# Conv weights of a lag stored side by side, v staged in filter slots, and a new job order, in a fused attention and long-convolution kernel

## The chip, the cores and the metric

The kernel runs on one core of one Trainium2 chip. The metric is the device time of one execution in microseconds (us). I call the engines PE (matmuls; PEld is its weight load), DVE (vector), ACT (scalar), POOL and SP, as the profile does. PSUM is the memory, in banks, that the matmuls write. The chain is the profile's path of work and waits that ended last. On one core an execution counts as slow when it lies over 1.5% above the fastest of the same kernel. A ratio is the mean time of one kernel's fast runs over the mean of the other's fast runs of the same rounds, so it is not quite the ratio of the medians that I quote beside it.

## The reference

Two independent parts, side by side in the output:

```python
# A: attention, S = 2048, D = 512, 32 heads of 16
qkv = (x @ wqkv).reshape(B, S, 3, H, Dh)
p = softmax(q @ k.T * Dh ** -0.5);  a = (p @ v) @ wo
# B: a short conv of 4 taps on k, times v, then a causal conv over the whole sequence, per channel
kv = short_conv(k, shift_k) * v
y = irfft(rfft(kv, 2 * S) * rfft(ssm_k, 2 * S))[:S] + kv * ssm_D
b = q * y
return concatenate([a, b], axis=-1)
```

## The kernel before

A Python scheduler emits one static program. Step T is one exponential on ACT over 2 or 3 banks of scores (741 steps). Between them PE does scores, p@v, projections and pieces of the conv; DVE computes 213 further score blocks by a polynomial (four passes each: FX, then EH, EH, EH or PTD) and empties PSUM.

The long conv is a matmul. For a channel, the 128 rows of `WR` hold the filter shifted by 0 to 63 places, once for each of two channels; the weights of a lag are up to 32 columns of `KV` (products of short conv and v). Four channels go to four column groups of the array at a time:

```python
KVF = sb("KV", [128, 2, 2 * NB, C // 2])          # channel innermost: a lag's weights are 512 bytes apart
KV = KVF[:, :, :, :].rearrange("p r (e h) u -> p r e h u", h=2)
...
# conv_lags: one lag, four channels c
ins = e.matmul(PS[32 * c:32 * c + 32 - 2 * q, BGB, 128 * kk:128 * kk + w],
               lhsT=KVF[:, lag % 2, 2 * q:32, 4 * od + c],
               rhs=WR[:, rows[c], w0:w0 + w],
               start=(n == 0), stop=(n == NLAG - 1), tile_position=(0, 32 * c))
...
# evac_unit, kind "kv": v was loaded into KV itself, and is multiplied in place
dst = KV[64 * p:64 * p + 64, i // 4, 4 * (i % 4):4 * (i % 4) + 4, p, 128 * c:128 * c + 128]
e.tensor_tensor(dst, src, dst, ALU.mult)           # src is PSUM; 32 of these, 64 x 512 each
```

`WR` has five slots of two channels. When a group of four channels is done, two slots are refilled, each by two transfers of 512 KB:

```python
def load_wr():
    while wr_free and wr_next[0] < 2 * NOCT:
        (i, dep), x = wr_free.pop(0), wr_next[0]
        ...                                          # cut
        for h in range(2):
            h_wr[x] = dma(sp, d_wr[i], WR[64 * h:64 * h + 64, 2 * i:2 * i + 2, :], src, [h_kzw[0], dep])
```

The softmax here doesn't subtract the row's maximum and nothing guards it: scores larger than these inputs give would overflow.

## Time and profile before

| | before |
|---|---|
| time, median of 4 | 987.3 us (982.4 to 991.3) |
| ACT, DVE, PE busy | 93%, 88%, 83% |
| mean PE clock granted | 0.944 |
| mean length of a DVE pass EH<-EH,FX | 781 ns |
| mean length of a product (L399) | 733 ns |

The lines themselves stand in the prediction. For the stages I count exponentials: step 60 ends at 82.4 us, step 184 at 230.9 us, step 740 at 978.6 us. So three stages: up to step 60 (projections alone), steps 60 to 184 (the products are made here) and steps 184 to 740 (attention with the conv, the long stage). From the trace I also add up, for each stage, the time at half PE clock, and the *fetch stalls*: gaps over 0.6 us in which PE has nothing in progress and for which a packet of the instruction queue ran in the 3 us before or during the gap. Such sums come from one profiled execution of each kernel.

### The profile page before, as it was taken

How to read it: one execution, taken by the hardware profiler on the slowest of the kernel's cores; microseconds unless marked ns; L12 is line 12 of the kernel's file. 1: busy time of each engine (PE TensorE's matmuls, PEld its weight loads, DVE VectorE, ACT ScalarE, POOL GpSimd, SP SyncE). 2: the span in 40 equal slices, each digit the busy share in tenths (PEclk: the TensorE clock that was granted, in tenths of full speed). 3: DMA queues.
4: the chain of work that ended last, by engine and by line, in shares of the span. 5: the costliest groups of instructions: out<-in, count | busy, mean ns of one | idle time of the engine just before them, and what ended most of it. 6: DMA issues, size and time to landing. Idle time of an engine off the chain costs nothing.

```text
span 985.5 us, 29568 instructions
## 1 busy us (share of the span) xinstructions
PE 814.5 (83%) x13348; PEld 376.9 (38%) x13389; DVE 865.7 (88%) x1330; ACT 912.0 (93%) x746; POOL 32.3 (3%) x35
## 2 busy tenths in 40 slices
PE   7888989888888888788887878877778888888877
PEld 2223233444344434344343344444444444333332
DVE  3238799999989999889899898999989999999993
ACT  5998799999989999989898899999989999999997
POOL 7000000000000000000000000000000000000000
PEclk9997599999989999989799799999989999999999
DMA  9990003538788988977788798887978977776502
GB/s 262 246 203 1 1 8 97 114 87 197 169 184 200 192 180 178 205 166 172 163 191 178 167 235 201 188 182 178 206 162 189 195 169 171 175 155 145 121 2 65
DMA packets 68013, 155.14 MB, mean 157 GB/s; under 512 B 31152, under 2 KB 33200, under 8 KB 67504
## 3 DMA queue, kind: packets, MB, share of 16 engines
q1 hardware_dynamic: 62624, 145.12, 66.4%
q0 software_dynamic: 1808, 6.29, 2.3%
q8 instruction: 106, 1.74, 0.8%
q10 hardware_dynamic: 3456, 1.84, 0.7%
q14 instruction: 19, 0.16, 0.1%
HBM read 142.61 MB, written 6.42 MB: 151 GB/s over the span
## 4 chain that ended last, share of the span: by engine, by line
ACT 46%; DVE 24%; PE 21%; issue 6%; SPq 1%; DMA 1%; ACTq 0%
ACT PT L555 46%; DVE EH L598 11%; PE PS L544 8%; PE PS L812 5%; PE PS L637 5%; DVE FX L591 4%; DVE PTD L603 4%; DVE KV L399 2%; PE PS L361 1%; DVE QT L386 1%; DVE DT L701 1%; SPq L221 1%; DMA WR<-in_B_ssm_D_dram 1%; PE PS L754 1%; PE PS L340 1%
## 5 line engine op out<-in xcount | busy, mean ns | idle before, releaser
L555 ACT ACTIVATE PT<-PS 128x1536 bf16<-128x1536 f32 (+1 forms) x741 | 908.9, 1424 | 61.5 <-PE PS L544 59.0
L544 PE MATMUL PS<-QT,KTo 32*128 32x512 bf16 x2048 | 316.9, 403 | 95.8 <-ACT PT L555 71.3
L598 DVE SCALAR_TENSOR_TENSOR EH<-EH,FX 128x512 f32<-128x512 f32 x426 | 320.3, 781 | 0.3
L812 PE MATMUL PS<-WR,KV 128*26 128x128 bf16 (+8 forms) x8192 | 286.2, 245 | 36.5 <-issue 35.0
L812 PEld LDWEIGHTS PS<-WR,KV 128*22 128x22 bf16 (+7 forms) x8192 | 231.9, 152 | 122.6 <-issue 100.6
L637 PE MATMUL PS<-PT,VAF 128*32 128x512 bf16 x1835 | 213.4, 409 | 13.0 <-issue 6.5
L591 DVE TENSOR_SCALAR FX<-PS 128x512 f32<-128x512 f32 x213 | 160.0, 751 | 30.5 <-PE PS L544 29.7
L544 PEld LDWEIGHTS PS<-QT,KTo 32*128 32x128 bf16 x2048 | 74.2, 91 | 268.7 <-ACT PT L555 216.1
L603 DVE SCALAR_TENSOR_TENSOR PTD<-EH,FX 128x512 uint16<-128x512 f32 x213 | 163.2, 771 | 0.3
L598 DVE SCALAR_TENSOR_TENSOR EH<-FX 128x512 f32<-128x512 uint16 x213 | 160.6, 774 | 0.1
L637 PEld LDWEIGHTS PS<-PT,VAF 128*32 128x32 bf16 x1835 | 49.7, 94 | 139.4 <-issue 121.4
L1012 PE MATMUL PS<-IDN,ZW 128*32 128x256 bf16 (+3 forms) x245 | 81.0, 331 | 0.7 <-DVE QN L845 0.4
L637 PE MATMUL PS<-PTD,VAF 128*32 128x512 bf16 x213 | 65.9, 407 | 0.0
L701 DVE STREAM_TRANSPOSE DT<-PS 128x512 f32<-128x512 f32 x31 | 23.1, 745 | 18.4 <-PE PS L637 18.2
L410 DVE CAST VAF<-PS 128x512 bf16<-128x512 f32 x16 | 11.1, 691 | 28.3 <-PE PS L369 28.3
L1012 PEld LDWEIGHTS PS<-IDN,ZW 128*32 128x32 bf16 x245 | 27.3, 112 | 5.8 <-issue 5.3
L399 DVE TENSOR_TENSOR KV<-PS,KV 64x512 bf16<-64x512 f32 x32 | 23.5, 733 | 3.7 <-PE PS L361 3.1
L386 DVE TENSOR_SCALAR QT<-PS,MASK 128x512 bf16<-128x512 f32 x30 | 21.4, 752 | 5.9 <-PE PS L340 5.7
L221 POOL DMA_DIRECT2D out_dram<-OUTA x12 | 7.1, 588 | 576.7 <-DVE OUTA L763 576.7
L369 PE MATMUL PS<-WKV,xT 128*128 128x512 bf16 x59 | 18.1, 391 | 6.0 <-DVE VAF L410 4.9
L754 PE MATMUL PS<-WKV,OTN 128*128 128x512 bf16 x50 | 16.9, 393 | 3.8 <-issue 1.9
L391 DVE CAST KTo<-PS 128x512 bf16<-128x512 f32 (+1 forms) x16 | 11.7, 732 | 8.8 <-PE PS L349 8.8
(63 smaller groups left out, 233.7 us busy)
## 6 DMA issues: line engine op xcount, KB each, us to landing
WR<-kz_scratch SPq DMA_DIRECT2D x256, 512.0 KB, 8.7
kz_scratch<-WR SPq DMA_DIRECT2D x1, 2176.0 KB, 8.5
KV<-in_B_v_dram SPq DMA_DIRECT2D x8, 256.0 KB, 6.1
QN<-in_B_q_dram POOLq DMA_DIRECT2D x2, 1024.0 KB, 11.5
out_dram<-QN POOLq DMA_DIRECT2D x2, 1024.0 KB, 7.2
out_dram<-OUTA POOLq DMA_DIRECT2D x12, 128.0 KB, 6.1
QN<-in_B_ssm_k_dram SPq DMA_DIRECT2D x1, 1024.0 KB, 6.2
QT<-in_B_ssm_k_dram SPq DMA_DIRECT2D x1, 1024.0 KB, 8.1
```

What stands on the lines that cost most here:

```text
L386: lambda e, par=par: e.tensor_scalar(QT[:, qb % 2, 2 * o + par, :], PS[:, bank, :], MASK[:, par:par + 1], None, ALU.mult),
L399: h_kvc[c] = hh = urgent(lambda e, dst=dst, src=src: e.tensor_tensor(dst, src, dst, ALU.mult), [h, h_vn[2 * c + i // 4], h_kv0], us=V512)
L544: ins = e.matmul(PS[:, bank, :], lhsT=KTo[32 * s:32 * s + 32, g // 2, kt * 128:(kt + 1) * 128], rhs=QT[32 * s:32 * s + 32, qb % 2, g, :], ...
L555: h_exp[T] = act.op(lambda e: e.activation(PT[:, T % R_PT, 0:n * QB], PS[:, banks[0]:banks[0] + n, :].rearrange("p b f -> p (b f)"), ACT.E ...
L591: h_f = urgent(lambda e: e.tensor_scalar(fx, PS[:, bank, :], FIX_ADD, FIX_HI, ALU.add, ALU.min), [h, h_last.get(i - R_FX)], slack=0.6)
L598: st["h"] = dve.op(lambda e: e.scalar_tensor_tensor(eh, src, (A3, A2, A1)[j], frac, ALU.add, ALU.mult), [st["h"], h_last.get(i - R_EH), h_ ...
L603: lambda e: e.scalar_tensor_tensor(out16, eh, A4, fx, ALU.mult, ALU.add),
L637: ins = e.matmul(dst, lhsT=w, rhs=rhs, start=(k == 0), stop=(k == KT - 1), tile_position=(0, 32 * s))
L701: h_t = urgent(lambda e: e.transpose(out=dt, in_=PS[:, pvb(n), :]), [h] + before, slack=0.1, us=(0.63, 0.751))
L754: ins = e.matmul(PS[:, bank, :], lhsT=OTN[:, (4 * qb + o) % R_O, t * 128:(t + 1) * 128], rhs=WO[:, o, :], start=(o == 0), stop=(o == 3))
L812: ins = e.matmul(PS[32 * c:32 * c + 32 - 2 * q, BGB, 128 * kk:128 * kk + w], lhsT=KVF[:, lag % 2, 2 * q:32, 4 * od + c], rhs=WR[:, rows[c] ...
L1012: pe.op(lambda e: e.matmul(PS[32 * s:32 * s + 32, pvb(n), 0:128 * k], lhsT=ZW[:, :], rhs=rhs, start=False, stop=False, tile_position=(0, 3 ...
```

## The change

The intent: bring a lag's weights next to each other (2 bytes apart instead of 512), so that weight loads are short. v can then no longer be loaded into its place by DMA in useful runs, so it is staged in two of the five filter slots, which come free when the last product is done. The job scheduler was changed with it.

```diff
-    KVF = sb("KV", [128, 2, 2 * NB, C // 2])
-    KV = KVF[:, :, :, :].rearrange("p r (e h) u -> p r e h u", h=2)
+    KVF = sb("KV", [128, C // 2, 2, 2 * NB])
+    KV = KVF[:, :, :, :].rearrange("p u r (e h) -> p r e h u", h=2)
+    VST = WR[:, 6:10, :]...                         # (cut) v, as [64 h, c, r, block, 128]
-    ld = dma(sp, d_kv[2 + 2 * c + r], KV[64 * h:64 * h + 64, r, :, h, 128 * c:128 * c + 128], src, kb=512)
+    ld = dma(sp, d_kv[2 + 2 * c + r], VST[64 * h:64 * h + 64, c, r, :, :], src, kb=512)
-    for h in range(2):                              # two memsets of 64 rows become one of 128
-        h_kv0 = pool.op(lambda e, h=h: e.memset(KV[64 * h:64 * h + 64, :, :, 1 - h, :], 0.0), ...)
+    h_kv0 = pool.op(lambda e: e.memset(KVF[:, :, :, :], 0.0), [h_vaf1], us=(14.0, 14.1))
-    e.tensor_tensor(dst, src, dst, ALU.mult)
+    e.tensor_tensor(dst, src, val, ALU.mult)        # val = the staged v
-    wr_free.extend([(i, h_kzw[0]) for i in range(R_W // 2)])   # at the start: five slots
+    wr_free.extend([(i, h_kzw[0]) for i in range(3)])          # now three
+    wr_free.extend([(3, hh), (4, hh)])              # after the last product
-    lhsT=KVF[:, lag % 2, 2 * q:32, 4 * od + c],
+    lhsT=KVF[:, 4 * od + c, lag % 2, 2 * q:32],
 # job order (N_EARLY is 184; cut to what differs)
+    if N_EARLY - 8 <= T < N_EARLY: return None      # no later job in the last 8 early steps
-    jobs.append((NT * (u[0] + 2) // NQB, ("op",) + u))
+    jobs.append((NT * (u[0] + 2) // NQB - SLOT, ("op",) + u))
-    if T >= stop:                                   # a job of which half is done
+    if T >= stop or N_EARLY - 3 <= T < N_EARLY:
-    if T < due and not fits(...): return
+    if not fits(...):                               # at most one forced job half per step
+        if T < due or forced and N_EARLY <= T < stop: return
+        forced = True
```

More of the change, by code (lines that the diff above doesn't have):

```diff
@@ L195, in bass_concat_heads__mha_block__ssm_conv_h3__prompt_kernel @@
     WO = WV
+    VST = WR[:, 6:10, :].rearrange("p c (r e d) -> p c r e d", r=1, e=NB).rearrange("p (c r) o e d -> p c (r o) e d", r=2)
     KZS = WRF[:, 0:4 * LKZ].rearrange("p (c m) -> p c m", c=4)
@@ L312, in bass_concat_heads__mha_block__ssm_conv_h3__prompt_kernel @@
     h_vaf1 = pool.op(lambda e: e.memset(VAF[:, :, H * VW:VROW], 1.0))
-    h_kv0 = h_vaf1
-    for h in range(2):
-        h_kv0 = pool.op(lambda e, h=h: e.memset(KV[64 * h:64 * h + 64, :, :, 1 - h, :], 0.0), [h_kv0], us=(4.5, 4.6))
+    h_kv0 = pool.op(lambda e: e.memset(KVF[:, :, :, :], 0.0), [h_vaf1], us=(14.0, 14.1))
     h_kz0 = pool.op(lambda e: e.memset(KZS[:, :, S:S + PAD], 0.0), [h_kv0])
@@ L397, in evac_unit @@
                 dst = KV[64 * p:64 * p + 64, i // 4, 4 * (i % 4):4 * (i % 4) + 4, p, 128 * c:128 * c + 128]
+                val = VST[64 * p:64 * p + 64, c, i // 4, 4 * (i % 4):4 * (i % 4) + 4, :]
                 src = PS[64 * p:64 * p + 64, bank, :].rearrange("p (b d) -> p b d", b=4)
-                h_kvc[c] = hh = urgent(lambda e, dst=dst, src=src: e.tensor_tensor(dst, src, dst, ALU.mult),
+                h_kvc[c] = hh = urgent(lambda e, dst=dst, src=src, val=val: e.tensor_tensor(dst, src, val, ALU.mult),
                                        [h, h_vn[2 * c + i // 4], h_kv0], us=V512)
@@ L405, in evac_unit @@
                 h_kvm[0] = h
+                wr_free.extend([(3, hh), (4, hh)])
+                load_wr()
         else:
@@ L880, in next_unit @@
             return early[0]
+        if N_EARLY - 8 <= T < N_EARLY:
+            return None
         if st["turn"]:
@@ L903, in unit_step @@
             return
+        forced = False
         while True:
@@ L923, in unit_step @@
                 free = max(free, at(*unit_deps(u)) + 0.13)
-            if T < due and not fits(T, free, 0.33 if u[0] == "turn" else 0.645 if u[0] == "kv" else 0.535):
-                return
+            if not fits(T, free, 0.33 if u[0] == "turn" else 0.645 if u[0] == "kv" else 0.535):
+                if T < due or forced and N_EARLY <= T < stop:
+                    return
+                forced = True
             if u[0] == "turn":
```

## The prediction

> **What bounds the kernel now.** I read the page first (busy shares, the slices, the chain that ended last), then the groups with shapes kept apart, the waits, the timeline around one ordinary burst and one stall, and the windows by stage. From the page:
>
> ```profile
> PE 814.5 (83%) x13348; PEld 376.9 (38%) x13389; DVE 865.7 (88%) x1330; ACT 912.0 (93%) x746; POOL 32.3 (3%) x35
> ...
> PEclk9997599999989999989799799999989999999999
> DMA  9990003538788988977788798887978977776502
> ...
> ACT 46%; DVE 24%; PE 21%; issue 6%; SPq 1%; DMA 1%; ACTq 0%
> ACT PT L555 46%; DVE EH L598 11%; PE PS L544 8%; PE PS L812 5%; PE PS L637 5%; DVE FX L591 4%; DVE PTD L603 4%; DVE KV L399 2%; PE PS L361 1%; DVE QT L386 1%; DVE DT L701 1%; SPq L221 1%; DMA WR<-in_B_ssm_D_dram 1%; PE PS L754 1%; PE PS L340 1%
> ```
>
> No engine bounds it alone. The exponentials on ACT (L555) are the backbone, 93% busy and 46% of the chain; the chain then hops to DVE (a quarter) and to PE (a fifth). The conv (L812), which the change is about, is only 5% of the chain, although it has 8192 of the 13348 matmuls. The ACT idle that could be won back is the waits' first ACT line, 59.0 us in all; a different view, the windows by stage, puts 43 us of idle (600 less 556.8 us busy) between 250 and 850 us, where DVE is as full as ACT:
>
> ```profile
> ACT PT L555 <- PE PS L544: 59.0, 82, 3.2
> PE PS L812 <- issue: 35.0, 26, 3.3
> ...
> 250.00:850.00 600.00, 489.41 (x9172) 246.21 (x9184) 558.84 (x848) 556.78 (x437) 8.84 (x13) 0.94 0.83 184
> ```
>
> Much of this idle is not conv time but PE standing still with no releaser. One such stall in the timeline:
>
> ```profile
> 256.68 0.23 PE L812 MATMUL PS<-WR,KV 128*4 128x128 bf16 x3 [2.62 <-issue]
> ```
>
> Reading the packets with the timeline, I find 31 PE stands over 0.6 us between 230 and 920 us with an instruction packet landing in or shortly before them, 44 us together. The half-clock spells (0.94 mean clock in that window) mostly begin a few us after such a stall.
>
> **What the Trainium skill says, and whether this trace agrees.**
> (1) "SBUF — State Buffer", section Door 1: The DMA port swizzle, has a note on lines: SBUF is read in 16-byte lines, and each access that crosses to a new line pays. The old weights of a lag lie 512 bytes apart, every one on another line; the new ones are 2 bytes apart. The trace agrees in direction: strided conv weights rise from 88 ns (2 columns) to 227 ns (30), while 32 contiguous columns of VAF take 94 ns:
>
> ```profile
> L812 PEld LDWEIGHTS PS<-WR,KV 128*30 128x30 bf16 x512 | 28.4, 227 | 6.2 <-issue 5.8
> L812 PEld LDWEIGHTS PS<-WR,KV 128*16 128x16 bf16 x512 | 18.1, 146 | 6.3 <-issue 5.1
> L812 PEld LDWEIGHTS PS<-WR,KV 128*2 128x2 bf16 x512 | 13.0, 88 | 8.8 <-issue 5.4
> L637 PEld LDWEIGHTS PS<-PT,VAF 128*32 128x32 bf16 x1835 | 49.7, 94 | 139.4 <-issue 121.4
> ```
>
> (2) "TensorE: Matmul & The Clock Gate", section Wait — 56ns, not 53.3ns?: back-to-back matmuls of 128 columns start 55.6 ns apart. Four column tiles at once make an estimate of 14 ns each. The trace agrees for narrow weights, below.
> (3) "Runtime: NRT & Kernel Launch", section Instruction fetch mechanics: instructions come in 16 KiB blocks of 256 by the engine's own DMA. The page's queue q8 shows 106 packets and 1.74 MB, so 16 KB each; that this is "mostly hidden", as the page has it, disagrees with the 2.62 us stall above. The change leaves the instruction count nearly alone, so this part of the idle should stay.
>
> **The change part by part.**
> *Weight layout.* A burst of conv matmuls on the timeline, as start, length and count:
>
> ```profile
> 478.98 0.89 PE L812 MATMUL PS<-WR,KV 128*20 128x128 bf16 x24
> 480.50 0.71 PE L812 MATMUL PS<-WR,KV 128*14 128x128 bf16 x24
> 482.22 0.42 PE L812 MATMUL PS<-WR,KV 128*6 128x128 bf16 x16
> ```
>
> The last matmul of each lasts 0.22 us, so the starts are (0.89-0.22)/23 = 29 ns apart at about 20 columns, 21 ns at 14, 13 ns at 6. Over all bursts of 18 to 24 at full clock the medians by mean width are 14 ns at 4 to 11 columns, 15.5 at 12 to 15, 19 at 16 to 19, 22 at 20 to 23, 25.5 at 24 to 27 and 29.5 at 28 and more. Contiguous, I expect 14 to 15 ns at all widths. There are 512 matmuls of each width: seven narrow widths save about 0.5 ns each, two save 5, two 8, two 11.5, three 15.5, in all 99 ns, times 512 = **51 us of PE time**. The 30-column load should fall from 227 to about 95 ns, PEld from 377 to some 270 us.
> How much lies on the path: adding up the chain's pieces, 1292 conv matmuls stand on it, 45.9 us, or 16% of 8192. So 0.16 x 51 = 8 us; the wide lags are likelier to be late, I choose **10 us**. The rest of the 51 us becomes PE waiting for ACT or DVE.
> *Staged v.* The 32 products (L399) now write with a step of 128 bytes and read v from the filter slots. They were
>
> ```profile
> L399 DVE TENSOR_TENSOR KV<-PS,KV 64x512 bf16<-64x512 f32 x32 | 23.5, 733 | 3.7 <-PE PS L361 3.1
> ```
>
> and read PSUM at one element per step anyway; I expect 730 to 800 ns. The chain holds 23 of them, so it costs 0 to 1.5 us, I take 1.
> *Zeroing.* Two POOL memsets of 6.9 us over 64 rows become one over 128 rows and twice the length, still 14 us, done by 18 us; the first product is at 84.9 us. Zero.
> *Slots.* Two of five filter slots stay taken until the last product, near 205 us. The order of instructions shows it: conv matmuls issued before exponential step 180 fall from 512 to 432. DMA is at 0.46 share from 125 to 250 us, so it has room; the 80 are made up later, spread over 540 steps, 80 x 15 ns = 1.2 us, mostly hidden. Zero to 1.
> *Job order.* The last four Q projections of the second block, which stood crowded at steps 170 to 194 with the k.v products, now spread to 236; output projections move some 20 to 40 steps later. All counts stay: 741 exponentials (353 and 388), 213 blocks on DVE, four passes each; warming matmuls 245 to 243; the conv ends at step 723 instead of 724. Each forced step carries one half job (about 0.5 us of PE) less. DVE QT is 10 us of the chain; taking a third of that stage's share gives **3 us**, a guess at the size.
> *Knock-on.* Shorter bursts bring the scores matmul (L544) sooner after ACT frees its bank and should save perhaps one half-clock spell: 2 us.
> Sum: -10 +1 +0.5 -3 -2 = -13.5 us, from 987.5 to **974 us**, 1.4%.
>
> **Rivals.**
> *PE is hidden anyway (DVE takes over).* For: DVE 558.8 of 600 us in the long stage, and 24% of the chain; FX must read a score bank before PE may refill it. Then the 51 us turn into PE idle and the time is 982 to 987. Against: the chain has 120 separate conv pieces, so PE was often the late one.
> *PE matters more than the chain's share.* When PE is late at one step, the next exponential, the DVE block and the bank all move, and the kernel's order was laid out for conv lags at 55 ns for four, which the wide ones exceed twofold. Contiguous weights would bring the order back into step with what runs; then half of the 51 us comes back, and 955 to 962 us result. For: DVE and ACT both show some 7% of slack in the long stage. Against: some 44 us of that goes with instruction fetch, which stays.
> *Fetch and clock get worse.* PE runs through its 256 instructions faster in a burst, so it may stand waiting for the next block just as long, now with less matmul work around it, and drop to half clock more often. Against: the mean rate over the kernel hardly moves. Time then 980 to 995. A slower strided write in the products (say 1 us each) would add 32 x 0.3 = 10 us at most, beside this.
>
> **Range and chances.** The three runs of before lie 9 us apart, and the throttle's half-clock spells move between executions, so +-5 us comes from this alone. From the middle case, the second rival reaches down to 957, the first and third up to 988. Two per cent faster is below 968: I give that 0.33, mostly the second rival; slower by over 2% (above 1007) needs the third rival at full size, 0.04; the rest 0.63.
>
> **What would show it.** Right: L812 loads near 95 ns at every width with PEld under 290 us; wide bursts at 14 to 16 ns; L812 at 3% of the chain or less; ACT idle before L555 down from 61.5 to about 48 us, with ACT busy and all counts unchanged. Products at 730 to 800 ns. PE stalls at issue still over 0.6 us some 30 times. Wrong: wide loads still above 150 ns (the stride was not the cause, the column count was); or short loads with ACT idle unchanged (DVE took over: a larger DVE share of the chain); or fewer fetch stalls and half-clock spells than before, which would make the gain larger by a step that I left out.

## The result, and the profile after

The changed kernel takes **1054.1 us** (median of 4, 1050.6 to 1056.8) against 987.3 us; the ratio is 1.068 (95% interval 1.061 to 1.074). It is correct. The prediction of 974 us was wrong, and 1054 us is far outside its range.

The page of the changed kernel, the lines that answer to those of the prediction (busy shares; PE clock and DMA in 40 slices; the chain that ended last):

```profile
PE 854.8 (81%) x13388; PEld 333.1 (32%) x13388; DVE 851.4 (81%) x1330; ACT 858.4 (81%) x746; POOL 31.1 (3%) x34
...
PEclk9897585866589898899898978779999879898899
DMA  9940001321498798898787888978778778788602
...
PE 37%; ACT 31%; DVE 21%; issue 8%; DMA 2%; SPq 1%; ACTq 0%; DVEq 0%
ACT PT L557 31%; PE PS L546 13%; PE PS L639 8%; PE PS L814 8%; DVE KV L399 7%; DVE EH L600 6%; DVE FX L593 3%; PE PS L360 2%; DVE PTD L605 2%; DMA WR<-kz_scratch 2%; PE PS L339 2%; PE PS L1019 1%; PE PS L756 1%; SPq L222 1%; DVE DT L703 1%
```

ACT fell from 93% to 81% busy. The products (KV, L399) rose from 2% to 7% of a longer chain, and the PE clock is at 5 to 8 tenths in every slice from the fourth to the twelfth, where before it was so in two of them. The windows by stage put the loss in one place. The columns are the stretch and its length, then busy time of PE, PEld, DVE, ACT and POOL with instruction counts, the PE clock, the DMA share and GB/s. First before, steps 60 to 184 and 184 to 740:

```profile
83.00:231.00 148.00, 132.95 (x1791) 56.72 (x1796) 137.36 (x217) 135.53 (x125) 2.08 (x2) 0.90 0.27 62
231.00:979.00 748.00, 611.23 (x11132) 300.58 (x11156) 692.64 (x1055) 704.20 (x556) 10.68 (x15) 0.95 0.77 171
```

then the changed kernel, the same steps:

```profile
86.00:300.00 214.00, 163.57 (x1707) 58.86 (x1704) 189.34 (x216) 136.17 (x125) 2.09 (x2) 0.66 0.20 45
300.00:1048.00 748.00, 615.85 (x11249) 254.56 (x11246) 627.30 (x1056) 649.98 (x556) 10.05 (x15) 0.89 0.78 173
```

Two things are to be seen. The stage with the products grew from 148 to 214 us, with the same 125 exponentials and 136 us of ACT work in it: that is nearly the whole loss of 67 us. And the long stage took 748 us in both, although DVE and ACT were busy 65 and 54 us less in it. So there is a large loss in one stage, and in the other a gain that went missing.

The loss is easy to find in the groups (mean ns after the comma) and on the timeline around 170 us. The groups of the changed kernel:

```profile
L399 DVE TENSOR_TENSOR KV<-PS,WR 64x512 bf16<-64x512 f32 x32 | 78.2, 2444 | 8.5 <-PE PS L360 8.0
L814 PEld LDWEIGHTS PS<-WR,KV 128*30 128x30 bf16 x512 | 13.7, 106 | 8.4 <-issue 7.3
```

its timeline (start, length, instruction, count, and the idle time before it with its releaser):

```profile
164.73 4.91 DVE L399 TENSOR_TENSOR KV<-PS,WR 64x512 bf16<-64x512 f32 x2 [0.86 <-PE PS L360]
169.69 0.53 PE L360 MATMUL PS<-OTN,QN 128*64 128x128 bf16 x6 [3.60 <-DVE KV L399]
```

and its waits:

```profile
ACT PT L557 <- PE PS L546: 180.5, 188, 4.4
PE PS L360 <- DVE KV L399: 26.1, 10, 3.9
```

A product takes 2444 ns instead of 733. The next short conv on PE needs the bank that the product reads, so PE stands for 3.6 us; PE's scores come late, and ACT waits 180.5 us for them in all instead of 59.0. By the windows above, 65 us of ACT's added idle lie in this stage; the other 54 lie in the long stage, which has no products. The weight load of 30 columns, on the other hand, did fall from 227 to 106 ns.

The missing gain shows in a view of one line of code: shortest, median and longest duration of a DVE pass. Before, then after:

```profile
L598 DVE SCALAR_TENSOR_TENSOR EH<-EH,FX x426: 616/710/1437, 78.9 to 964.1; 128x512 f32<-128x512 f32 x142
```

```profile
L600 DVE SCALAR_TENSOR_TENSOR EH<-EH,FX x426: 623/681/693, 82.3 to 1031.5; 128x512 f32<-128x512 f32 x142
```

These passes touch neither PE nor the conv's data, and yet the long ones, up to 1437 ns, are gone. I took it that something in the old weight loads had slowed DVE; e7 and e8 below test it. Why did that bring no time in the long stage? There the time at half clock rose from 75 to 167 us and the fetch stalls from 31 with 44 us to 46 with 73 us.

### The profile page after: what moved, and what is told of

The parts are those of the page before. It is cut to its first block, busy times and chain, and to the rows that moved or that the text cites. A ratio compares the mean times of both kernels' runs of the same rounds, so it can differ in the third digit from the quotient of the medians.

```text
span 1054.9 us, 29610 instructions
## 1 busy us (share of the span) xinstructions
PE 854.8 (81%) x13388; PEld 333.1 (32%) x13388; DVE 851.4 (81%) x1330; ACT 858.4 (81%) x746; POOL 31.1 (3%) x34
## 4 chain that ended last, share of the span: by engine, by line
PE 37%; ACT 31%; DVE 21%; issue 8%; DMA 2%; SPq 1%; ACTq 0%; DVEq 0%
ACT PT L557 31%; PE PS L546 13%; PE PS L639 8%; PE PS L814 8%; DVE KV L399 7%; DVE EH L600 6%; DVE FX L593 3%; PE PS L360 2%; DVE PTD L605 2%; DMA WR<-kz_scratch 2%; PE PS L339 2%; PE PS L1019 1%; PE PS L756 1%; SPq L222 1%; DVE DT L703 1%
## 5 line engine op out<-in xcount | busy, mean ns | idle before, releaser
L557 ACT ACTIVATE PT<-PS 128x1536 bf16<-128x1536 f32 (+1 forms) x741 | 855.3, 1269 | 183.9 <-PE PS L546 180.5
L546 PE MATMUL PS<-QT,KTo 32*128 32x512 bf16 x2048 | 347.0, 436 | 85.0 <-ACT PT L557 43.7
L814 PE MATMUL PS<-WR,KV 128*30 128x128 bf16 (+8 forms) x8192 | 265.1, 237 | 47.5 <-issue 40.7
L600 DVE SCALAR_TENSOR_TENSOR EH<-EH,FX 128x512 f32<-128x512 f32 x426 | 280.5, 678 | 0.4
L639 PE MATMUL PS<-PT,VAF 128*32 128x512 bf16 x1835 | 233.4, 443 | 17.4 <-DVE DT L703 8.0
L814 PEld LDWEIGHTS PS<-WR,KV 128*18 128x18 bf16 (+7 forms) x8192 | 173.9, 97 | 157.7 <-issue 125.9
L605 DVE SCALAR_TENSOR_TENSOR PTD<-EH,FX 128x512 uint16<-128x512 f32 x213 | 143.6, 678 | 0.2
L1019 PE MATMUL PS<-IDN,ZW 128*32 128x512 bf16 (+3 forms) x243 | 83.4, 343 | 4.1 <-issue 4.1
L399 DVE TENSOR_TENSOR KV<-PS,WR 64x512 bf16<-64x512 f32 x32 | 78.2, 2444 | 8.5 <-PE PS L360 8.0
L339 PE MATMUL PS<-xT,WQ 128*128 128x512 bf16 x60 | 24.6, 507 | 3.1 <-DVE KV L399 2.2
```

Source lines behind the costliest of these rows:

```text
L339: return e.matmul(PS[:, bank, :], lhsT=WQ[:, dc, o * 128:(o + 1) * 128], rhs=xT[:, dc, qb * 512:(qb + 1) * 512], start=(dc == 0), stop=(dc ...
L399: h_kvc[c] = hh = urgent(lambda e, dst=dst, src=src, val=val: e.tensor_tensor(dst, src, val, ALU.mult), [h, h_vn[2 * c + i // 4], h_kv0], ...
L546: ins = e.matmul(PS[:, bank, :], lhsT=KTo[32 * s:32 * s + 32, g // 2, kt * 128:(kt + 1) * 128], rhs=QT[32 * s:32 * s + 32, qb % 2, g, :], ...
L557: h_exp[T] = act.op(lambda e: e.activation(PT[:, T % R_PT, 0:n * QB], PS[:, banks[0]:banks[0] + n, :].rearrange("p b f -> p (b f)"), ACT.E ...
L600: st["h"] = dve.op(lambda e: e.scalar_tensor_tensor(eh, src, (A3, A2, A1)[j], frac, ALU.add, ALU.mult), [st["h"], h_last.get(i - R_EH), h_ ...
L605: lambda e: e.scalar_tensor_tensor(out16, eh, A4, fx, ALU.mult, ALU.add),
```

## The experiments

My theory after the result: (A) the product's write with a step of 128 bytes is the loss. The rival (B): the two missing filter slots and the job order are. Then, for the long stage: what ate the gain of the short weight loads? All runs gave the reference's result except the two that say otherwise. The order of instructions on every engine is exactly the same in the changed kernel, e1 to e4, e7 and e8, in e6, e10 and e11, and in e12 and before, except for the operands named and, where transfers are held or left out, those waits and transfers. At the mark of 2% the changed kernel is slower, e7, e8, e10 and e11 are faster and e6 is the same; e1 to e5 and e12 are on record as unclear. Smaller differences I read by the interval.

### e1: only the layout put back

```diff
-    KVF = sb("KV", [128, C // 2, 2, 2 * NB])         # and the views that go with it
+    KVF = sb("KV", [128, 2, 2 * NB, C // 2])
```

> The changed kernel with only the layout of the weights put back (a lag's weights 512 bytes apart, the products written in runs of 128 elements); v still staged in filter slots, job order as changed. Theory A (the products' write with a step of 128 bytes is the loss): the product falls from 2.44 to about 0.7 us, wide weight loads go back to some 220 ns, steps 60 to 184 take 148 us instead of 214, the time is 985 +-10 us. Rival B (two filter slots missing and the new job order are the loss): it stays above 1040 us with products at 0.7 us.

Measured: 999.1 us, ratio to before 1.020 (1.010 to 1.031). The lines that decide:

```profile
L399 DVE TENSOR_TENSOR KV<-PS,WR 64x512 bf16<-64x512 f32 x32 | 23.2, 725 | 5.2 <-PE PS L360 4.6
L814 PEld LDWEIGHTS PS<-WR,KV 128*30 128x30 bf16 x512 | 28.5, 222 | 5.9 <-issue 5.7
```

Steps 60 to 184 take 146 us, as before the change. Theory A holds and B falls as the main cause: staging and job order were still in. But 999 is 4 us above what A allowed, and the excess lies in the long stage (764 us). That remainder is taken up in e5.

### e2, e3, e4: channels in groups of 8, 4 and 2

A middle way between the layouts: `s` channels next to each other, so that weights are 2s bytes apart and the product writes runs of s elements.

```diff
-    KVF = sb("KV", [128, C // 2, 2, 2 * NB])
+    KVF = sb("KV", [128, C // 2 // s, 2, 2 * NB, s])
-    lhsT=KVF[:, 4 * od + c, lag % 2, 2 * q:32]
+    lhsT=KVF[:, (4 * od + c) // s, lag % 2, 2 * q:32, (4 * od + c) % s]
```

> The changed kernel with channels in groups of 8: a lag's weights 16 bytes apart, the products written in runs of 8 elements (16 bytes). Theory A: products near 0.7 us if a run of 16 bytes is enough, 1 us at most; wide weight loads as slow as at 512 bytes (about 220 ns) if every weight on another 16-byte line is what costs, near 100 ns if it is the size of the step. Time 980 to 995 us. Rival B: above 1040 us.

> Groups of 4: weights 8 bytes apart (two on a 16-byte line), product runs of 8 bytes. If cost goes by 16-byte lines: products between 0.7 and 1.4 us, wide weight loads between 100 and 160 ns. Theory A: 985 to 1010 us. Rival B: above 1040 us.

> Groups of 2: weights 4 bytes apart (four on a line), product runs of 4 bytes. Theory A: products about 1.2 to 1.6 us, wide weight loads about 100 to 120 ns, time 1000 to 1025 us. Rival B: above 1040 us.

| | weights apart | load of 30 columns | run of a product | product | time (median) | ratio to before |
|---|---|---|---|---|---|---|
| changed kernel | 2 bytes | 106 ns | 1 element | 2444 ns | 1054.1 us | 1.068 |
| e4 | 4 bytes | 104 ns | 2 elements | 686 ns | 982.0 us | 1.001 (0.987 to 1.014) |
| e3 | 8 bytes | 115 ns | 4 elements | 686 ns | 981.2 us | 1.002 (0.993 to 1.012) |
| e2 | 16 bytes | 145 ns | 8 elements | 686 ns | 983.7 us | 1.004 (0.994 to 1.015) |
| e1 | 512 bytes | 222 ns | 128 elements | 725 ns | 999.1 us | 1.020 (1.010 to 1.031) |

The four share one set of runs of before, whose fast ones were three of seven (973 to 982 us). The profile of e2 fell in a slow execution; only its instruction lengths are used. A pair is enough: 4 bytes written together take the product from 2444 to 686 ns. My expectation of 1.2 to 1.6 us for pairs was a miss, so the cost does not go by the bytes written together. Two smaller misses: e2's weight load, 145 ns, lies between its two cases, and e3 ran 4 us below its range.

```profile
L400 DVE TENSOR_TENSOR KV<-PS,WR 64x512 bf16<-64x512 f32 x32 | 22.0, 686 | 2.5 <-PE PS L361 2.0
L815 PEld LDWEIGHTS PS<-WR,KV 128*30 128x30 bf16 x512 | 13.6, 104 | 7.8 <-issue 6.5
```

These are e4's lines: short weight loads and a fast product together. Against e1, with one and the same order of instructions, the layout gives 17 us by the medians. Yet e4 is no faster than the kernel before.

### e9: the write by itself

Twelve products of 64x512 from PSUM behind everything else, with nothing beside them, in different write and read patterns.

```diff
+    for name, dims in forms:
+        h_m[0] = dve.op(lambda e, dims=dims, views=views: e.tensor_tensor(ap(0, dims), views(P64), views(A64), ALU.mult), ...)
```

> The kernel before with twelve products of 64x512 put behind everything else, when no other engine works, in this order: eight that write, in elements of 2 bytes, runs of 512; single elements with a step of 2, 4 and 16 elements; the changed kernel's pattern (single, steps 2 and 64); pairs with a step of 4 and of 32; runs of 4 with a step of 64; then three that read these patterns (run of 512, step 16, the changed pattern) and write plainly; then one that writes single fp32 elements 16 bytes apart. If an isolated 2-byte write is what costs (e4's pairs were fast): about 0.69 us for all writes but the four single ones, which take 2.4 us whatever the step; reads and fp32 near 0.7 us. If it is 16-byte lines: step 2 and 4 stay near 0.7 to 1.4 us, step 16 and the changed pattern 2.4 us, fp32 at 16 bytes slow too. The kernel's own time is no longer of use.

The timeline, one write pattern per line: single elements with a step of 2, 4 and 16 elements (4, 8, 32 bytes), the changed kernel's pattern, pairs every 8 bytes, pairs every 64 bytes:

```profile
991.91 0.72 DVE L1068 TENSOR_TENSOR xT<-PS,KTo 64x512 bf16<-64x512 f32 x1
992.66 1.28 DVE L1068 TENSOR_TENSOR xT<-PS,KTo 64x512 bf16<-64x512 f32 x1
993.98 2.29 DVE L1068 TENSOR_TENSOR xT<-PS,KTo 64x512 bf16<-64x512 f32 x1
996.30 2.43 DVE L1068 TENSOR_TENSOR xT<-PS,KTo 64x512 bf16<-64x512 f32 x1
998.76 0.68 DVE L1068 TENSOR_TENSOR xT<-PS,KTo 64x512 bf16<-64x512 f32 x1
999.48 0.68 DVE L1068 TENSOR_TENSOR xT<-PS,KTo 64x512 bf16<-64x512 f32 x1
```

The changed pattern costs 2.43 us with nothing else running, so neither contention nor the staged v is needed to explain it. Both of my ideas of the law were wrong in part: single 2-byte elements cost more the wider the step (0.72, 1.28, 2.29 us), which "isolated elements" alone did not say; and pairs cost nothing even 64 bytes apart, where each falls on another 16-byte line, which "lines" did not say. Reading v in the changed pattern instead of writing it took 1.00 us, and single fp32 elements written 16 bytes apart 1.03 us.

### e5: the job order alone, and e6: groups of two with the old job order

```diff
 # e5: the kernel before, plus only the five job-order hunks of the change
 # e6: e4, minus those five hunks
```

> The kernel before with the job order of the change alone (layout and v as before). e1 was 999 us where before was 990. Theory C (the new job order costs the 1 to 2%): 995 to 1005 us, with the loss in steps 184 to 300. Rival D (the staging of v in two filter slots costs it): within 5 us of before.

> Groups of two (e4) with v staged, but the job order of before. Theory C: e4 was 982 us, this gives 968 to 975 us and beats both kernels. Rival D: 980 to 985 us, as e4.

e5 took 1003.6 us, ratio 1.018 (1.013 to 1.024): the job order by itself costs what e1 was too slow by, and staging v costs nothing that these runs can see (the intervals leave room for some 10 us, and with two slots more the same rules give e5 another order of instructions than e1). The long stage is 764 us in e5 and in e1, 748 us before. In e5 the excess is spread: 7 us of it in steps 184 to 300, 9 us after. Which of the five hunks does it stays open. e6 took **973.3 us**, ratio 0.990 (0.985 to 0.995), one per cent less than before and 81 us less than the changed kernel. With groups of two the old order gains 9 us by the medians (e4 to e6), half of what it is worth in e5, though the intervals overlap.

### e7 and e8: the filters loaded once (wrong result)

e4 and e1, in which each slot is loaded the first time and never again; the matmuls read what is there. The matrix of four cells (two layouts, with and without transfers) tells what the layout is worth when nothing else disturbs.

```diff
-    h_wr[x] = dma(sp, d_wr[i], WR[...], src, [h_kzw[0], dep])
+    if first: slot_h[i] = h_wr[x] = dma(...)         # later loads: no transfer; the conv waits on the first one's semaphore
```

> Wrong result on purpose: e4 in its exact order of instructions, but each filter slot is loaded once and not again, so that nearly all transfers of the long stage are gone. Theory E (the instruction blocks come late because they queue behind filter transfers, and the half-clock spells follow from those stalls): the 40 fetch stalls of steps 184 to 740 fall under 10, the half-clock time there from some 170 us to under 50, the time by 50 us or more, to 910 to 935 us. Rival F (the stalls are not due to the transfers): unchanged within 10 us.

> As e7 with the old layout of the weights (e1 without reloads), wrong result on purpose. Together with e7 it gives what the weight loads alone are worth when no transfer disturbs. Theory E with the prediction's 10 to 17 us for the layout: 10 to 25 us longer than e7. If fetch stalls and the clock ate a larger gain in e4 against e1, the difference here is over 25 us; if DVE hides it, under 8 us.

e7 took 869.1 us (0.882 of before, 0.876 to 0.888) and e8 951.6 us (0.967, 0.960 to 0.973). So with transfers the layout is worth 17 us (e1 to e4), and without them **82 us** (85 if e7's two slow runs are left out). e8's main expectation, 10 to 25 us, was a miss; its second case, over 25 us, holds. A DVE pass in e8 and then in e7:

```profile
L603 DVE SCALAR_TENSOR_TENSOR EH<-EH,FX x426: 615/717/1401, 82.5 to 933.5; 128x512 f32<-128x512 f32 x142
```

```profile
L604 DVE SCALAR_TENSOR_TENSOR EH<-EH,FX x426: 627/687/709, 82.7 to 852.3; 128x512 f32<-128x512 f32 x142
```

Sorting the EH and PTD passes by what PE does beside them shows one reason. In e8 a pass with no conv weight load beside it takes 0.69 us on average, and one with more than 1.5 us of weight loads beside it (added up over parallel loads) takes 0.94 us. In e7 both take 0.69 us. Before it is 0.69 and 0.93 us. The loads with a step of 512 bytes slow DVE by a third while they run; those with a step of 4 bytes do not. In e8 DVE stood for 51% of the chain that ended last, in e7 for 38%.

DVE is not the only one. ACT's exponentials, the backbone of the chain, also took less time without the strided loads. Here are all 741 in e8 and then in e7:

```profile
L560 ACT ACTIVATE PT<-PS 128x1536 bf16<-128x1536 f32 (+1 forms) x741 | 905.0, 1454 | 36.8 <-PE PS L549 35.9
```

```profile
L561 ACT ACTIVATE PT<-PS 128x1536 bf16<-128x1536 f32 (+1 forms) x741 | 836.2, 1368 | 27.0 <-PE PS L550 26.1
```

ACT is busy 69 us less (DVE 76 us less, 864.0 to 787.7). Sorted in the same way, an exponential over 1536 columns takes 1.79 us in e8 beside many weight loads and 1.52 us beside none, in e7 1.62 and 1.52 us. Which share of the 82 us each engine carries was not separated.

The expectation was a fall by 50 us or more, and it was 113 us from e4 to e7. Fetch stalls in the long stage fell from 43 with 81 us to 6 with 5 us, half-clock time from 171 to 10 us. (e7's profile is of a slow execution, 878 us, at a mean clock of 0.969; the fast ones had 0.984 to 0.992.) Rival F falls. But e7 takes away both the traffic and the queueing, which e10 and e11 separate.

### e10, e11, e12: all filters loaded, but at most two or three transfers in flight

Every transfer has its own semaphore, and SP issues a transfer only when the one two (three) before it has landed. The same bytes move. e10 and e11 start from e6, e12 from the kernel before.

```diff
+    h_wr[x] = dma(sp, d_wr[2 * i + h], WR[...], src, [h_kzw[0], dep],
+                  hold=wr_all[-3:][:1] if len(wr_all) >= 3 else ())
+    wr_all.append(h_wr[x])
```

> e6 (973 us) in its exact order, but a filter transfer (512 KB) is issued only when the one two before it has landed, so that at most two stand before an instruction block in the queues. Theory E (blocks queue behind filter transfers): fetch stalls of steps 184 to 740 fall from 69 to under 25 us, half-clock time from 178 to under 90 us, total 925 to 955 us. If two in flight are too few for the rate (11 us for the four of an octet), PE waits for filters instead and it is slower than e6.

> As e10 with three in flight. Theory E: between e6 and e10, 945 to 970 us, fetch stalls 30 to 55 us. If the number in flight has no part in it: 973 us.

> The kernel before in its exact order and layout, with at most three filter transfers in flight as in e11. If the freed fetch is the whole gain of e11: 890 to 905 us. If the old layout still slows the vector passes beside it (0.92 against 0.69 us in e8 and e7), this ends near e8, 945 to 965 us, and e11 is over 50 us faster: then the layout is worth that much once the blocks arrive in time.

| | time (median) | ratio to before | long stage | half clock in it | fetch stalls in it |
|---|---|---|---|---|---|
| before | 987.3 us | 1 | 748 us | 75 us | 31, 44 us |
| changed | 1054.1 us | 1.068 | 748 us | 167 us | 46, 73 us |
| e1 old layout | 999.1 us | 1.020 | 764 us | 109 us | 35, 52 us |
| e4 groups of 2 | 982.0 us | 1.001 | 754 us | 171 us | 43, 81 us |
| e6 groups of 2, old order | 973.3 us | 0.990 | 742 us | 178 us | 37, 69 us |
| e10: e6, two in flight | 955.9 us | 0.970 (0.964 to 0.975) | 720 us | 137 us | 20, 43 us |
| **e11: e6, three in flight** | **892.0 us** | **0.906 (0.899 to 0.912)** | 659 us | 31 us | 16, 20 us |
| e12: before, three in flight | 955.7 us | 0.972 (0.962 to 0.982) | 723 us | 24 us | 20, 23 us |

e11 is much faster than I expected (945 to 970 us). Its first ACT wait, its long window and its filter transfers (the last number is the median from issue to landing; it was 8.7 us before):

```profile
ACT PT L558 <- PE PS L547: 31.4, 41, 4.7
```

```profile
250.00:800.00 550.00, 468.31 (x9795) 203.59 (x9791) 533.14 (x906) 534.70 (x467) 8.91 (x14) 0.98 0.96 213
```

```profile
WR<-kz_scratch SPq DMA_DIRECT2D x256, 512.0 KB, 7.2
```

The DMA moves 213 GB/s there, more than the 184 GB/s of before in its window, and still the stalls fell from 69 us in e6 to 20 us: the traffic was not the trouble, but how much of it was queued at once. Two in flight are too few. e10's chain is 72% filter transfers, and PE waits for filters, as its expectation allowed for. In e6 PE's longest wait was one with no releaser, in e10 it is this one:

```profile
PE PS L815 <- issue: 61.7, 36, 5.0
```

```profile
PE PS L821 <- DMA WR<-kz_scratch: 54.7, 32, 6.5
```

It is still faster than e6, which that sentence had not allowed for. By my count its stalls (43 us, not under 25) and its half-clock time (137 us, not under 90) were misses. But that count takes any gap with a packet near it, and "near" covers about half of the long stage. A sharper count takes only the gaps over 0.6 us of the long stage for which the profile shows no releaser ("issue"); in every run all of these end 1.15 to 1.85 us after an instruction packet has ended. There are 26 with 39 us before, 39 with 65 us in the changed kernel, 34 with 66 us in e6, 11 with 13 us in e12, 8 with 12 us in e11, and none in e7, e8 and e10. In e10 22 gaps with 51 us end with a filter transfer instead. So the fetch stalls fell at each step from e6 to e11 to e10, and what held up e10 instead were waits for filters.

e12 shows that the limit alone, on the kernel before, gives 2.8% (1.8 to 3.8%). The layout on top of it, with e6's staging and e6's order of instructions, gives the other 64 us (955.7 to 892.0).

## Why the prediction was wrong, point by point

- **Staged v** is the step that failed. The prediction put it as "I expect 730 to 800 ns" and "it costs 0 to 1.5 us", and its third rival capped a slower write at "32 x 0.3 = 10 us at most". The product measured 2444 ns (e9: 2.43 us with nothing beside it). That is 32 x 1.71 = 55 us of DVE time, in a stage where PE needs the bank back; the stage grew by 65 us, with 147 us of it at half clock instead of 31. The reasoning "read PSUM at one element per step anyway" looked at the read side only. e1 takes the loss away by putting the whole layout back, e4 by writing pairs while its weight loads stay short; what the two share is the fast write.
- **Job order**, predicted as a gain of 3 us "a guess at the size", costs 18 us in the old layout (e5: 1.8%). The sign was wrong. Why is open.
- **Weight layout**: the load itself came out as predicted (30 columns: 106 ns against "about 95"; the matmuls of a burst now start 11.5 to 13 ns apart in the median at every width, against "14 to 15"). But PEld fell only to 333 us in all ("some 270"), and the conv rose to 8% of the chain ("3% or less"). The chosen 10 us compares with 17 us from e1 to e4. But the term left out was larger than the one counted: the strided loads slowed DVE passes by a third and lengthened ACT's exponentials. In the changed kernel's long stage the job order (16 us in e5) and the third rival then took this gain away: "Fetch and clock get worse" was right about the direction (31 to 46 stalls, 75 to 167 us at half clock). That faster bursts are the reason was not shown, and its "against: the mean rate over the kernel hardly moves" was beside the point.
- **Slots** and **zeroing**: right. e1 and e5 differ by nothing that can be told apart (1.020 and 1.018), and the memset took 13.75 us and delayed nothing.
- **Fetch stalls** "some 30 times" were 46 in the long stage, and the half-clock spells grew with them instead of shrinking; the 2 us of "knock-on" went the other way. Stall and half-clock spell fall together in e7 (171 to 10 us at half clock) and e11 (178 to 31 us); that the one causes the other was not tried separately. In e10, and in the changed kernel while it makes its products, PE stood for other reasons and half-clock time was long too (137 and 147 us), so it is not tied to instruction fetch alone.
- **The second rival** (PE and its layout matter more than the chain's share) was right in substance but for another reason, shorter DVE passes and exponentials, and needed e11's limit to show: 82 us without transfers, 64 us with them.

What stays open: which job-order hunk costs the 18 us; what makes single 2-byte writes dear and pairs not; how DVE and ACT share the gain of the layout; and how in detail an instruction packet is held up behind filter transfers (its own length does not show it: 1.3 us in the median in e6 and in e11).

## What to carry to other kernels

When a layout is changed for its reader, time the writer too: here one more element per run (pairs instead of singles) kept the whole gain of the reader and took the write from 2.4 us to 0.7 us. When an engine stands still with no releaser and instruction packets land just then, look at how many bulk transfers are in flight; here a limit of three gave 81 us (e6 to e11), and only with it did the better layout pay in full. And compare the same instruction with and without another engine's work beside it: a strided weight load on PE showed up as a slow pass on DVE and a longer exponential on ACT.

## What the Trainium skill lacked or had wrong

- "SBUF — State Buffer", Door 1: The DMA port swizzle: the note on 16-byte lines does not foretell the write. Pairs of bf16 64 bytes apart, each on another line, took 0.68 us for 512 elements, as a plain run does; single elements 4, 8 and 32 bytes apart took 0.72, 1.28 and 2.29 us. For weight loads it gives the direction, but the cost goes on rising past a line: 30 columns took 104, 115, 145 and 222 ns at steps of 4, 8, 16 and 512 bytes.
- "SBUF — State Buffer", Who interferes with whom: it says that only the port pair shared by DVE and GpSimd causes contention. DVE passes beside weight loads with a step of 512 bytes took 0.93 to 0.94 us against 0.69 us without, and 0.69 us beside those with a step of 4 bytes. ACT was busy 905 us with the former and 836 us with the latter for the same 741 exponentials (e8, e7).
- "Runtime: NRT & Kernel Launch", Instruction fetch mechanics: crossing a block is called mostly hidden. It cost 44 us in 31 stalls of the long stage before, and 20 us with at most three transfers in flight (39 and 12 us by the sharper count).
- "DMA: Bandwidth & Descriptors", Queues, rings and completion order: from its round robin between queue rows, packet by packet, I would not have expected that it matters to an instruction block how many filter transfers are queued. From e6 to e11 the fetch stalls fell from 69 to 20 us and the time from 973 to 892 us by that number alone, with the same bytes moved.
